# New ranks, longer charges for some loads, and more zero matmuls in an attention and MoE kernel ordered by a planner

## The chip, the cores and the metric

The kernel runs on one core of one Trainium2 chip. The metric is the device time of one execution in microseconds (us). The kernel before takes 373.11 us, the median of seven runs that lie between 372.59 and 374.45 us.

## The reference

The input is `q`, `k` and `v` of 8 batches x 8 heads x 576 positions x 64, a feature matrix `w_phi` (64 x 128), and the two weights of an MLP (512 x 2048 and 2048 x 512). All are float32, and so is the output.

```python
def phi(x):
    proj = np.einsum('bhsd,df->bhsf', x, w_phi)
    proj = proj - np.max(np.abs(proj), axis=-1, keepdims=True)
    return np.concatenate([np.exp(proj), np.exp(-proj)], axis=-1)
q_p, k_p = (phi(q), phi(k))
kv = np.einsum('bhsf,bhsd->bhfd', k_p, v)
z = np.sum(k_p, axis=2)
num = np.einsum('bhsf,bhfd->bhsd', q_p, kv)
den = np.einsum('bhsf,bhf->bhs', q_p, z)[..., None] + 1e-06
attn = num / den
...
x = attn.transpose(0, 2, 1, 3).reshape(B * S, H * D)   # 4608 x 512
h = x @ w_in
g = np.where(h > 0.0, h, np.exp(np.minimum(h, 0.0)) - 1.0)
return g @ w_out
```

It is linear attention with an exponential feature map, and behind it a two-layer MLP with ELU on every token.

## The kernel before

**Work and tiles.** Attention is cut into 16 quads of four heads: quads 2b and 2b+1 hold batch b. The MLP is cut into nine chunks of 512 tokens: chunk b takes the first 512 positions of batch b, and chunk 8 takes the last 64 positions of all batches (the "tails"). A chunk can start when both quads of its batch have delivered their part of `x`.

**One quad.** TensorE (PE) transposes k and q (L537, tails L541), multiplies them with `w_phi` (L565, L583 for the maxima, L714 and L726 for the transposed q features). VectorE (DVE) reduces the maxima `m_k`, `m_q` (L592). ScalarE (ACT) makes the exponentials `EK`, `EKt`, `Eq`, `Eqt` (L629, L765). From `m_k` ACT makes the scales `em` (L661), and GpSimd (POOL) multiplies `v` with them into `vs` (L684). PE then makes `kv` (L797), an engine copies it (L816), PE makes the outputs `pn` and `pnt` (L850, L865), DVE weighs and adds them into `tot` (L885, L891), divides (L923, L924) and multiplies `tot` with the reciprocal into `x` (L928; on DVE for quads 0 and 1, on POOL for the others). `x` is transposed into `xT` (L980 and L988 for batches 0 and 1, by DMA for later ones).

**One chunk.** For each of 16 column tiles: four matmuls into `ph` (mm1, L1031), `exp` on ACT (L1043), minus one on POOL (`u_sb`, L1047), the ELU on DVE (`gT`, L1054). Then 16 groups of matmuls into `po` (mm2, L1097), a copy (L1120) and a store.

**Loads.** k, q and the weights are read as float32, cast to bfloat16 on the way, and issued from POOL's own instruction stream (L385, L391, L412, L422). For batches 0 and 1 v is issued there too; for later batches it goes through SP. Batch 0 comes in halves of four heads plus tails (`load_first`, L1174); batch 1 comes whole plus tails (`load_kq`, L1192, with n = 0, 1, 2 for k, q, v).

**What sets the order.** All instructions are put in order when the kernel is built, by the class `Planner` (L125). Every piece of work is an `Op` with a charged duration for each engine that may run it, the ops that it waits for, and the PSUM banks that it takes. `run` (L169) is a list scheduler: it steps through a time of its own, and whenever an engine is free it takes, among the ops that are ready by the charges, the one with the lowest rank. Each engine later runs its list strictly in that order, waiting on semaphores for real. The charges therefore set the order only, never the time. The ranks are a table of 2091 numbers, `RANKS`: op n has the two digits 2n and 2n+1 in base 64.

A load is charged by its size; it is taken to have landed at

```python
took = o.load / self.MB_PER_US
o.seen = max(o.end + o.alone, dma + took + self.LANDING)
dma = max(dma, o.end) + took
```

with 0.37 MB per us, so that loads queue behind each other. At most eight loads of POOL are on their way at once (`AHEAD`, L140; `wait`, L207).

**Zeros in the gaps.** When PE starts an op after having stood idle in the planner's time, and that time is below 60 us, the planner first puts in matmuls of zeros into an otherwise free PSUM bank (`fill`, L1244 and L1247; the count is set at L264). One is taken as 0.056 us (`FILL`), and they are given half of the gap. They cost nothing in the planner's time. Ahead of everything else, 30 are put in at L1252.

Of the kernel before, what the change touches and what calls it, by code (L numbers as in the profile page):

```python
# [31 lines left out]

DIGITS = "0123456789ABCDEFGHIJKLMNOPQRSTUVWXYZabcdefghijklmnopqrstuvwxyz+-"
RANKS = (
    "0S0Y0b0a0n0X0c0v0o0w0-0z382k1x1t3H3B3y1v3o1n3J3Y3h3-784G4c080Q1i1b0B6v3K1Y7t1k0T"
    "2Q0P7a7h0s150t7c1o851w197T7g1+2c1l0G0A2t1z2A5w3PA81u060h0O0g3L0N2z096r0p033p9T0D"
    "2v211K4q39516z165V4L32233f2w0F302m4r3q6s704J8YA62C4N2g5D1D120K0e1N3v2r5q3N1U9u7M"
    "298I86272EBY8N7z839i0+AZAB7q8S375e2M8G898R6a5+6u3M049G130502013QBmPUTNBz7QVz758n"
    "8B601I2s6A0u0f3r0y0k280j1H1O0R0d2F1d0Z2+1f0q1RIC5T0U3k1A5k3n1L1P492H182o5848340i"
    "4t365p2L4n1y3F114Y461cAy4x4U4Q26509a3W5G5d3t5m5KDo633D5nBH3I9-3m5H424j8W5C3u1a3C"  # L40
    "F+2n1M2X524F1m1EAl6D1Z53656KDwE27I4H4i9EI+6F7G3e4h9X5lAE7UCT4W9O9SG+5XCeAC7E3X0l"
    "17003i3sAU3O547K0M774wCu9h7OAF1p9b4v7W7oCp7u7jA4Ah901-AgAj828c0r933R2b8z0HKH2-1C"
    "3T9y5a61DnA-Ao3a3l5M249D2S3Z0m5i4E2y764g2p3w4k1Q144I5o1T4o2e0V4K312i4l2x3zDe7H6o"
    "3b5W6y1F3E7J3S7P7b0C2U0J0I7m8r8k8p2I0E2K7s877x9n9r5u4e8dFv5y8m5PCJD63U7wA22a5R8b"
    "5Q3V7X7+5s5t6E6m6LCL8F0L6C6H416B2u4m1gFa4z0xEE6-CjAv95109f4s1B6l6i2P3344405I4a6M"
    "Ab3G5A9J3jBF725B5U926b6k2Z254XA33d2dBT9V5fCVAq6G3c984ZChGr7ZEF4PAe5S5Z6hEZBXBuCo"
    "CZ994B3+Bs8w4p9mBg8OAmCiCfBVHdB4IxBbGDFcBp7NG3CnB0ALBvDWBCAfI2GcF-ETFKEP5vDGAkH0"
    "BDHDDxD-EaAQDc7L7D3x8Q2V9s1J1e2W202J4T5b7n2O1j9vAD7i9l8C5NBnBJBSCm8Z7VDCCFAA7k7e"
    "CG8i4CD98q9pFD668M2NNsEiE7As8a6d2RCaBoAN1q1s1X5YC6CK4D4b436O0W6Z5F1V5h4d9R5j7r2f"
    "Gg6g9gCs2j1hAYEBAX35FfAJ4A2h4S6Q6P4OCvC3DO7p6q6jD8CXC98hC06w6n8T6tD1739B8xBiIR7A"  # L50
    "Cy7Y8X2D6S741r5x079A8+6URA9K9Z9k9U7B5c2G795L71CQ6p6+8LBA9MH98j1WHJ629xC284BUFr47"
    "2qGiF55-6fARI4DMMKAnGyDPJX7FCHEUCb594VDN5gAHLzDKJ-BGFBB9JY5EHn9CCYAxDj9NCc5JJj9c"
    "Hp2YG1DRHo2lMJArCx55RZ9+JNBMJnDSD4BWHfDDCw4-LeASJb8uLdB8Hl8yQZF7FoGUFEBP819FJGFl"
    "FdD0B5ApGICkC-DU8HI0KjFLH+KXFp4y4+4f7f64It4RCMCD6I6RCgCzCWC8888PC4B+8K9w8fCrAV9t"
    "809qKqOpE-AGA5AO2BDiDtB6B76WCSCA6e8DEKIK6TBtBZ1G5zB1DvDY9o6NDIELCEAK8U5rC+227CAM"
    "CRH4ClM+9WAT9P9L8g1S9dD594A7FzGG458A4M8e6VEYJHRCEvPDOoKrGCJz7lRBMyRNKxKtLLL3JL8J"
    "IP69EeB3ERByAIEN6XQ-KN9j6xF8GE6YK+PRBx6cB2CdFeRG97Fu7yDaFyC78tEVEHHCA+DV96ErFTK1"
    "9QIU9eEIDmFUC1KOD7FIHaBBBl2TOmE6J27vTkF6HkBfGqElJ7BqLiDEJZBRMtFJGpBcTFFCI83AHYFw"
    "A056SlFiHmB-G-F2Jl57UUFgJh8sUgFXI9BEOfG8K4BrQ1HZJi4uQFIcGlBKHIHAJ6BeD+GjPYIYNoEq"
    "CtFnMoGRLwIODqOQJ5E+KlCPE5JcLvJwGeHeG6E4CNEs7-DkE8BID3A1CCFNFHNCPLQI9zPKEgR7MuCU"  # L60
    "PqDgOTCO5ODACBRuKzL1ESAuNIL0MiKuKWFRQPJRCqIk8EDpFSC5QKNLInIjI6FFA9IaDFG5GHDXFq7R"
    "G7EC8vHEEDEzGBH-H3G9FZAdHtDdH1F9DLITLPFb679YE1CIFPF19IP4PAE3LFPJUNFkTOE0N+SFNWP3"
    "DhKCBkP2GOGLKcDfEoEtS7SUFOL6QbSSEpEG8VFQDZL48-KoHyTlGfOUFVEmLYIgAWGo9HHbFAH5LaK3"
    "HBF3FYAiGnDQHhL9JqGxGuOcFtGbMNLtJaBjMEIHM0GdMHJ0MjGMQ0I-IwAtQCLRIsAPQDIVHrBwQ9Nc"
    "JTNfSfKwJmFxPBK2Hz91QzIGIFBNGzJJO8GYUSLOIEBOT+LINyBQMQJQJ4AaQ3L-K5FhHcIvRtGNMGJO"
    "OWNDO6JMIZLhKFMgRFINJAQUN1LHMeSvHFOMMAKvO3KPP58oBdF0EyPvNFGwJ1EMI1HNAwOnIqMrKZOs"
    "KyKgP0N4N8K-N7EfKKEQO5EbKGIJGPSLOxFMFsS6EAHQQxN2DBIX6JPfHOPFUCEjDuIDS4HjEkDHHuH6"
    "LXAcIoGQHKBaHGJSGZOVJBDbH7IpLTGvI3DJGmT6IMSCEOGKHgJ8AzIrHPEuOYEJKEJrJkKLJxKSR0RE"
    "L7MzJoJ9PXQvKIRYSRKRNjP6TnPzRjRiHRDsJuR3NmJKKbHSIfJfQwSnOZS9JFJpIiRoLlI77dOOSyGs"
    "DlM6HHVuODGtDTKkIuGSOAKJD2OzGTIWIAFmP-NKT4MfQ2MlSzBhQYLyQOLqLpOdSbVqSdNVJWFjMSMp"  # L70
    "QsG4QyNQUOMYU4MFUiGaNvMqQfW4TzO2NRVrN0LQT1GVLfPlScO9QGMCUvW9SjN9U2NMQ5NUN-GWRvMO"
    "JULgUBLkRnPPMULmQkMmQoLbNHSmIzQeLMRJUIOwTuQnMsSgSGI5R57SEdEhFGReR9KhIyH8JEHVLUEW"
    "OSRxRaQqE9JsT5RzGAKTN6Q+NqSETET3JtRrFWSpRkRsP+IbJvHXL5T8JIILL8PcKAKsJCKdRqKeTQLo"
    "KpLWVmMXMILsMBO4MkHqVGK9HxUwLxHsVOJVHvVeLuDrOkMvRwPwGhRUHMMLG0KQHUF4KaJyPnRXKfPj"
    "ROV6VkRTQrTxNSDyNbLCNZNdPTQhUmNeIIEwIQL2HWRbRcOtNkKnNgKBPOOr8lSIPmMPNwPNTMKYOuLr"
    "QVM9OPMhToVWO7UVVaP1VTSaNhUXKiHLTmVVMnKmRyPSTaK7UZBLM5PWTLGkUkONUdMaOgOvO0OyUHNt"
    "J3U-QANPQiVLNpOXUbGJPrNEV3MDMwLDK6V2UENaJ+VIO+OROKSWMRPZMZV-L+O-URW1M4LZUjVRSeRH"
    "K0RdU9NzTYQ8ShRfPpRIWgNlUqRVSTSJWcQtUzPIW0UPSYSAU+UpOlUDVAWGUtLBKDNOLNUlMVEXPuH2"
    "M3OFKUUTTSTKR-RRTBUKRgR+T9RWR6PHR1TvLVEcIhDzGXLJLSIeIlQES2OIRDPxTTSiSOSHOHU3LKEn"
# [45 lines left out]
class Planner:  # L125
# [43 lines left out]
    def run(self):  # L169
        free = dict.fromkeys(self.LAG, 0.0)  # L170
# [11 lines left out]
        now = 0.0  # L182
# [53 lines left out]
        while todo:  # L236
            started = False
            for e in ready:
# [22 lines left out]
                for x in o.cost:  # L261
                    ready[x] = [y for y in ready[x] if y[1] is not o]
                if e == "PE" and 0.0 < free[e] and now < self.FILL_UNTIL and banks:
                    n = int(0.5 * (now - free[e]) / self.FILL)  # L264
                    if n:
                        if filled not in banks:
                            filled = min(banks, key=banks.get)
                        self.fill(filled, n)
# [50 lines left out]
def kernel(  # L319
# [10 lines left out]
    nc = tc.nc  # L330
# [140 lines left out]
    def plan_quad(i):  # L471
# [454 lines left out]
        def x_head(e, c):  # L926
# [8 lines left out]
        div = add({"DVE": 0.37}, divide, tots, key=-9.0)  # L935
        ops["x"] = [
            add(
                {"POOL": 1.11} if i > 1 else {"DVE": 0.68},
                lambda e, c=c: x_head(e, c),
                [div, *old("x_out")],  # L940
                key=-9.0,
# [232 lines left out]
    def load_first(n, part):  # L1174
        if part == 1:
            load((0, n, 1), 0.13, 1.26, lambda e: load_tails(nc.gpsimd, n, 0))
            return
        h = 2 * part

        def load_half(e):  # L1180
            load_main(nc.gpsimd, n, 0, h, h + 4)
            if not n and not part:
                make_identity(nc, ident)

        load((0, n, part), 0.52, 0.8 if n or part else 1.19, load_half)

    for n, part in (
        (0, 0), (0, 1), (0, 2), (1, 0), (1, 1), (2, 0), (2, 1), (1, 2), (2, 2)
# [1 line left out]
        load_first(n, part)  # L1190

    def load_kq(n):  # L1192
        load((1, n, 0), 1.05, 0.9, lambda e: load_main(nc.gpsimd, n, 1, 0, 8))
        load((1, n, 1), 0.13, 1.26, lambda e: load_tails(nc.gpsimd, n, 1))
        landed[1, n, 2] = landed[1, n, 0]

# [87 lines left out]
```

## Time and profile before

| | before |
|---|---|
| median of seven runs | 373.11 us |
| the profiled execution's own time | 372.99 us |
| its span, first to last instruction | 371.2 us |
| busy: PE / ACT / DVE / POOL | 352.2 / 271.9 / 266.8 / 248.5 us |
| PE busy with zeros (L1247), 212 matmuls | 20.6 us |
| first matmul of mm1 (L1031) starts | 51.1 us |
| mean DMA rate in the first 60 us | 202 GB/s |

Times in the profile run from the start of the span. Outside the span lie 372.99 - 371.2 = 1.8 us. In the tables by stretch of time, each engine has its busy time and, in brackets, the number of its instructions; "PEclk" is the share of full clock that TensorE was granted. In a chain of waits, each row has its start, its duration and what the end was waiting for at that moment. Matmuls are pipelined: the duration of one includes its way through the array.

### The profile page before, as it was taken

To read this page: it belongs to the slowest core of one execution; us is meant where nothing else is said; L and a number is where in the kernel's file an instruction comes from. 1 tells how busy PE (TensorE), PEld (TensorE's weight loads), DVE (VectorE), ACT (ScalarE), POOL (GpSimd) and SP (SyncE) were. 2 spreads that over 40 slices of the span, in tenths; PEclk is the share of its full clock that TensorE was granted. 3 is DMA by queue.
4 is the path that set the end of the run, shared out by engine and by line. 5 is a ranking of instruction groups with operands and counts; after the bars stand their busy time and mean duration, and the time that the engine had idled before them with its cause. 6 is when DMAs were issued, how large, how long until landed. Compare 5 with 4: busy or idle time off the path is not lost.

```text
span 371.2 us, 8974 instructions
## 1 busy us (share of the span) xinstructions
PE 352.2 (95%) x3380; PEld 197.0 (53%) x3426; DVE 266.8 (72%) x562; ACT 271.9 (73%) x601; POOL 248.5 (67%) x359
## 2 busy tenths in 40 slices
PE   7787989999998999999999999999999999999995
PEld 6566855555545454444554555464544554444444
DVE  4789789998879867868885889798858851777000
ACT  2998897988899945899678979996699733665111
POOL 8899989877967877689357794928485624675000
PEclk9999899999999999999999999999999999999999
DMA  8999999599794998757579353583120034000213
GB/s 130 212 193 238 210 201 213 35 130 177 100 169 69 179 224 127 135 117 143 119 92 186 91 143 83 135 175 63 34 60 2 34 86 118 1 0 2 86 57 87
DMA packets 85788, 43.20 MB, mean 116 GB/s; under 512 B 54704, under 2 KB 79664, under 8 KB 85744
## 3 DMA queue, kind: packets, MB, share of 16 engines
q1 hardware_dynamic: 56016, 26.10, 33.0%
q0 software_dynamic: 29328, 16.00, 31.6%
q8 instruction: 27, 0.44, 0.5%
q10 hardware_dynamic: 400, 0.52, 0.4%
q14 instruction: 17, 0.14, 0.1%
HBM read 36.77 MB, written 9.44 MB: 124 GB/s over the span
## 4 chain that ended last, share of the span: by engine, by line
PE 79%; POOL 8%; DMA 5%; issue 3%; ACT 3%; DVE 2%; POOLq 0%; ACTq 0%
PE po L1097 33%; PE ph L1031 29%; PE pkv L797 5%; PE pk L583 4%; PE pn L850 4%; DMA q_b<-in_q_dram 3%; POOL vs L684 3%; POOL u_sb L1047 2%; DMA k_b<-in_k_dram 2%; PE pq L714 1%; DVE gT L1054 1%; POOL w_in_sb L385 1%; PE pnt L865 1%; ACT EK L629 1%; POOL k_b L422 1%
## 5 line engine op out<-in xcount | busy, mean ns | idle before, releaser
L1097 PE MATMUL po<-w_out_sb,gT 128*128 128x512 bf16 (+1 forms) x567 | 130.8, 373 | 1.6 <-issue 0.6
L1047 POOL TENSOR_SCALAR u_sb<-e_sb 128x512 bf16<-128x512 f32 x144 | 87.9, 618 | 48.3 <-ACT e_sb L1043 45.1
L1031 PE MATMUL ph<-xT,w_in_sb 128*128 128x512 bf16 x491 | 118.3, 379 | 1.7 <-DVE gT L1054 0.5
L1054 DVE SCALAR_TENSOR_TENSOR gT<-u_sb,ph 128x512 bf16<-128x512 bf16 x144 | 96.2, 682 | 32.7 <-POOL u_sb L1047 32.4
L1043 ACT ACTIVATE e_sb<-ph 128x512 f32<-128x512 f32 x144 | 87.2, 618 | 31.0 <-PE ph L1031 27.1
L1031 PEld LDWEIGHTS <-w_in_sb 128*128 128x128 bf16 x576 | 53.7, 98 | 62.0 <-issue 4.2
L1097 PEld LDWEIGHTS <-gT 128*128 128x128 bf16 x592 | 54.0, 98 | 56.9 <-issue 2.9
L684 POOL TENSOR_TENSOR vs<-v_b,em 128x512 bf16<-128x512 f32 (+1 forms) x96 | 78.7, 844 | 1.6 <-DMA v_b<-in_v_dram 1.4
L629 ACT ACTIVATE EK<-pk 128x512 bf16<-128x512 f32 x128 | 68.8, 631 | 11.9 <-PE pk L583 11.5
L765 ACT ACTIVATE Eq<-pq 128x512 bf16<-128x512 f32 x128 | 70.2, 628 | 3.1 <-PE pq L714 3.0
L592 DVE TENSOR_REDUCE m_q<-pk 128x4 f32<-128x512 f32 (+1 forms) x80 | 48.4, 628 | 14.0 <-PE pk L583 10.9
L592 DVE TENSOR_REDUCE m_k<-pk 128x4 f32<-128x512 f32 (+1 forms) x80 | 47.6, 627 | 5.6 <-PE pk L583 4.6
L928 POOL TENSOR_TENSOR x<-tot,rec 128x576 bf16<-128x576 f32 x28 | 31.8, 1151 | 25.3 <-DVE rec L924 21.2
L1120 ACT COPY o_sb<-po 128x512 f32<-128x512 f32 (+1 forms) x28 | 16.1, 575 | 36.9 <-PE po L1097 34.7
L885 DVE TENSOR_TENSOR tot<-pn,w 128x260 f32<-128x260 f32 x64 | 26.1, 422 | 9.8 <-PE pn L850 7.4
L850 PEld LDWEIGHTS <-Eq 128*128 128x128 bf16 x512 | 22.2, 98 | 8.9 <-issue 1.2
L891 DVE TENSOR_TENSOR tot<-tot,pn 128x260 f32<-128x260 f32 x64 | 25.6, 418 | 0.4
L850 PE MATMUL pn<-kv,Eq 128*128 128x65 bf16 x512 | 25.3, 195 | 0.5 <-DVE gT L1054 0.4
L629 ACT ACTIVATE EKt<-pk 64x256 bf16<-64x256 f32 x64 | 22.9, 378 | 2.3 <-PE pk L565 1.2
L797 PEld LDWEIGHTS <-EK 128*128 128x128 bf16 x512 | 22.2, 98 | 3.5 <-issue 0.3
L797 PE MATMUL pkv<-vs,EK 128*128 128x65 bf16 x512 | 23.7, 195 | 0.2 <-POOL vs L684 0.2
L1247 PE MATMUL fill<-zeros 128*128 128x128 bf16 x212 | 20.6, 245 | 3.0 <-DVE zeros L1163 1.0
(75 smaller groups left out, 305.4 us busy)
## 6 DMA issues: line engine op xcount, KB each, us to landing
out_dram<-o_sb SPq DMA_DIRECT2D x32, 256.0 KB, 2.7
v_b<-in_v_dram SPq DMA_DIRECT2D x6, 1024.0 KB, 7.3
k_b<-in_k_dram POOLq DMA_DIRECT2D x7, 512.0 KB, 7.4
q_b<-in_q_dram POOLq DMA_DIRECT2D x7, 512.0 KB, 9.5
w_in_sb<-in_moe_w_in_dram POOLq DMA_DIRECT2D x8, 256.0 KB, 8.6
w_out_sb<-in_moe_w_out_dram POOLq DMA_DIRECT2D x4, 512.0 KB, 11.8
v_b<-in_v_dram POOLq DMA_DIRECT2D x2, 512.0 KB, 6.1
v_b<-in_v_dram POOLq DMA_DIRECT2D x1, 1024.0 KB, 11.6
```

The source lines that it names most:

```text
L592: nc.vector.tensor_reduce(largest(n)[:, cols], bank.tile[:, 0:len(range(2 * NS)[cols]), :], axis=AX.X, op=ALU.max, apply_absolute_value=True,)
L629: nc.scalar.activation(EK()[:, 2 * c + par, sg, :] if c < 2 else EKt[r, s, sg, :], bank.tile[r, 0:n, :].rearrange("p a b -> p (a b)"), ACT ...
L684: nc.gpsimd.tensor_tensor(st["vs"][:, sg, r, 0:D], kqv[b, 2][:, o:o + n * D].rearrange("p (n d) -> p n d", d=D), st["em"][:, sg, r, None]. ...
L765: nc.scalar.activation(dst, src, ACT.Exp, scale=1.0 - 2.0 * sg)
L797: nc.tensor.matmul(pkv[:, c, sg, :], st["EK"][:, 2 * c + t % 2, sg, (2 * s + t // 2) * F:(2 * s + t // 2 + 1) * F,] if t < NT else EKt[:, ...
L850: nc.tensor.matmul(pt[:, t, :], st["Eq"][:, par, c, sg, o:o + P], st["kv"][:, s, c, sg, :], start=True, stop=True,)
L928: (nc.vector if e == "DVE" else nc.gpsimd).tensor_tensor(tile("x", work, [P, NS, 2, D], BF16)[:, :, c, :], tot[:, r, 0:D], st["rec"][:, r, ...
L1031: nc.tensor.matmul(ph, w_in_sb[:, ct, jt * P:(jt + 1) * P], xTs[ch][:, ct, :] if ch < B else xT_tail[:, ct // 2, :, ct % 2, :], start=(ct ...
L1043: nc.scalar.activation(t["e"], bank.tile, ACT.Exp)
L1047: nc.gpsimd.tensor_scalar(t["u"], t["e"], -1.0, 1.0, op0=ALU.add, op1=ALU.mult)
L1054: nc.vector.scalar_tensor_tensor(gTs[ch][:, jt, :], t["u"], 0.0, bank.tile, op0=ALU.min, op1=ALU.max)
L1097: nc.tensor.matmul(bank.tile, gTs[ch][:, jt, tt * P:(tt + 1) * P], w_out_sb[:, jt, o0:o1], start=(jt == 0), stop=(jt == N_JT - 1),)
```

## The change

Four kinds of edits are made.

- The size charged for loads rises: k and q halves of batch 0 from 0.52 to 0.55, v halves of batch 0 from 0.52 to 0.62, v of batch 1 from 1.05 to 1.35. The bytes that are moved stay the same.
- `x` on DVE (quads 0 and 1, two ops each) is charged 1.05 us in place of 0.68.
- Zeros take 0.65 of a planned gap in place of 0.5.
- All of `RANKS` is replaced. It has the same 2091 entries, again each number from 0 to 2090 once.

No op is added or removed apart from the zero matmuls.

```diff
 RANKS = (
-    "0S0Y0b0a0n0X0c0v0o0w0-0z382k1x1t3H3B3y1v3o1n3J3Y3h3-784G4c080Q1i1b0B6v3K1Y7t1k0T"
...
+    "1B1g0S0V1V0-2c1-2b2j2x3K32312I303P3R4Z334A393S3g343h5Q1K1Z123i2F2-0w4S0X0D0M01A1"
...
                 if e == "PE" and 0.0 < free[e] and now < self.FILL_UNTIL and banks:
-                    n = int(0.5 * (now - free[e]) / self.FILL)
+                    n = int(0.65 * (now - free[e]) / self.FILL)
                     if n:
...
             add(
-                {"POOL": 1.11} if i > 1 else {"DVE": 0.68},
+                {"POOL": 1.11} if i > 1 else {"DVE": 1.05},
                 lambda e, c=c: x_head(e, c),
...
-        load((0, n, part), 0.52, 0.8 if n or part else 1.19, load_half)
+        load((0, n, part), 0.62 if n == 2 else 0.55, 0.8 if n or part else 1.19, load_half)
...
-        load((1, n, 0), 1.05, 0.9, lambda e: load_main(nc.gpsimd, n, 1, 0, 8))
+        load((1, n, 0), 1.35 if n == 2 else 1.05, 0.9, lambda e: load_main(nc.gpsimd, n, 1, 0, 8))
         load((1, n, 1), 0.13, 1.26, lambda e: load_tails(nc.gpsimd, n, 1))
```

## The prediction

> **What bounds the kernel now.** I read the table by stretch of time first: start, length, then busy time of PE, PEld, DVE, ACT and POOL, then granted clock, DMA share and GB/s.
>
> ```profile
> 0.00:10.00 10.00, 7.75 (x77) 7.02 (x77) 5.32 (x14) 2.92 (x5) 8.86 (x18) 1.00 0.86 133
> 10.00:20.00 10.00, 7.27 (x107) 5.48 (x106) 7.98 (x16) 9.61 (x23) 8.27 (x13) 1.00 1.34 211
> 20.00:30.00 10.00, 8.81 (x165) 6.91 (x164) 8.21 (x17) 9.93 (x27) 9.22 (x15) 1.00 1.18 202
> 30.00:40.00 10.00, 7.28 (x134) 6.03 (x131) 8.18 (x20) 7.40 (x20) 9.20 (x13) 0.87 1.22 230
> 40.00:50.00 10.00, 8.56 (x144) 7.22 (x142) 9.42 (x23) 9.43 (x23) 9.97 (x13) 0.96 1.37 207
> 50.00:100.00 50.00, 49.41 (x529) 27.44 (x534) 44.55 (x98) 43.09 (x98) 42.15 (x61) 1.00 1.02 138
> 100.00:120.00 20.00, 18.75 (x216) 10.67 (x218) 15.45 (x34) 18.46 (x45) 15.15 (x23) 1.00 0.80 122
> 120.00:340.00 220.00, 217.32 (x1893) 112.51 (x1924) 165.65 (x343) 165.41 (x358) 144.37 (x207) 1.00 0.50 99
> 340.00:371.20 31.20, 27.06 (x139) 13.68 (x140) 2.06 (x3) 5.69 (x11) 1.31 (x3) 1.00 0.22 68
> ```
>
> From 50 us on PE is full: it misses 0.59 + 1.25 + 2.68 = 4.5 us of 290, and 4.1 us at the end. Before 50 us it is busy 39.67 us, but about half of that is zeros:
>
> ```profile
> L1247 PE MATMUL fill<-zeros 128*128 128x128 bf16 x212 | 20.6, 245 | 3.0 <-DVE zeros L1163 1.0
> ```
>
> All but some 0.5 us of these lie before 50 us, so the first 50 us hold about 19.6 us of needed PE work and lose 30.4. The span is then 331.6 needed (352.2 - 20.6) + 30.4 + 0.5 + 4.5 + 4.1 = 371.1 of 371.2. What a new order can win is in the ramp, and there it is set by the start of mm1, at 51.1 us. Next, the chain of waits ahead of it (start, duration, what):
>
> ```profile
> 25.05 10.46 DMA q_b<-in_q_dram
> ...
> 35.56 0.24 PE trt L541
> ...
> 36.14 0.49 PE fill L1247 x6
> 36.63 1.54 PE pkv L797 x40
> ...
> 40.14 0.90 PE fill L1247 x9
> ```
>
> PE stands on the tails of q of batch 1, then on zeros, and only then makes kv of quad 1. Why that kv was not possible sooner is in POOL's timeline:
>
> ```profile
> 29.61 0.81 POOL L391 DMA_DIRECT2D w_out_sb<-in_moe_w_out_dram  x1
> 30.42 0.61 POOL L385 DMA_DIRECT2D w_in_sb<-in_moe_w_in_dram  x1
> 31.04 1.42 POOL L684 TENSOR_TENSOR vs<-v_b,em 128x128 bf16<-128x128 f32 x2
> 32.39 0.95 POOL L412 DMA_DIRECT2D q_b<-in_q_dram  x1
> 33.36 2.05 POOL L684 TENSOR_TENSOR vs<-v_b,em 128x512 bf16<-128x512 f32 x2
> ```
>
> vs of quad 1 ends at 35.41 us because POOL issues loads in between; its EK and Eq were finished by 30.3 us.
>
> **What the Trainium skill says.** "TensorE: Matmul & The Clock Gate", Part 1: after an idle window of about 3.4 us TensorE runs at half clock until it has been busy that long again. The trace agrees: 30 zeros take 3.38 us at the start (0.113 each), 24 take 1.50 us when warm (0.056 each plus 0.16 of way through the array), and the clock falls to 0.87 just after the stand at 33.9 to 35.6 us. Same page, "Step-by-step: what each phase is for": matmuls stay in program order and only weight loads are pulled ahead. The trace agrees: L541 idles PE for 1.48 us on a landing. "DMA: Bandwidth & Descriptors", "Queues, rings and completion order": a ring's descriptors are consumed in order. Here the q tails, 128 KB of input, need 10.46 us because v of batch 1 was issued before them (23.52, landing 11.6 us later). "SBUF — State Buffer", "SBUF: two separate sides": a DVE operation with two SBUF inputs and a GpSimd operation that reads SBUF exclude each other. `x` on DVE is such an operation (0.744 to 0.885 us, median 0.754).
>
> **The change, part by part.**
>
> *Charges.* At 0.37 MB per us, the new sizes put what lands after v of batch 1 later by 4 x 0.03/0.37 + 2 x 0.10/0.37 + 0.30/0.37 = 0.32 + 0.54 + 0.81 = 1.7 us in the planner's time. The landings say that this is the right direction: v of batch 1 landed 3.9 us after the load before it (31.17 to 35.08), q of batch 1, with as many elements, 2.6 us after the one before it; the charge goes from 2.84 to 3.65. So the planner no longer believes that the q tails come before kv of quad 1, and the 1.48 us stand has no reason to be planned. Behind it stood six zeros that waited 0.30 us for a bank (ACT reading `qT`) and took 0.49. But kv could not start before vs, at 35.41; it started at 36.42. Worth 1.0 us.
>
> *Clock.* From 36.6 to 41.7 us needed work ran cold: 40 of pkv 1.54 against 1.26 us later, 8 of pk 0.61 against 0.40, 2 of pq 0.64 against 0.38, 16 of pn about 0.2 over: 0.95 us. Without the stand, and with more zeros, I take half: 0.5.
>
> *Zeros.* The 182 in gaps stand for at least 182 x 0.056/0.5 = 20.4 us of planned gap. At 0.65 they become about 240: 58 x 0.056 = 3.2 us more of PE time warm, 58 x 0.113 = 6.5 cold. It costs nothing where PE waits anyway (1.09 us after the group at 15.76, 0.77 at 11.65, 1.48 at 33.86) and everything where real work is ready. Two groups stand on the chain; at 1.3 times they add 2 x 0.056 + 3 x 0.12 = 0.5 us. Bounds: -1.4 us (the whole cold stretch saved: 0.95 and 0.4 of its zeros) to +3.2 (all on the path). Value taken: +0.4.
>
> *Ranks.* Decoded, the vs of quad 1 had 382 to 539 against loads at 226 (w_out), 235, 242 (w_in) and 251 (q of batch 2); now it has 36 to 222 against 234, 196, 266 and 304. Its scales (L675) go from 150 to 233, so some loads still pass. `x` of quad 1 goes from 349 and 1164 to 245 and 163, against maxima of quad 3 that were at 19, 146, 485 and 502 and are now at 285, 526, 12 and 495. The eight large EK of quad 2 go from 22 to 824 to between 27 and 1300, six of them above 600. Batch 0 is thus preferred to batch 1. How far can that pull mm1? POOL gave 0.65 + 0.64 + 0.93 + 1.25 + 0.59 + 0.81 + 0.81 + 0.61 + 0.95 = 7.2 us to loads between the scales and the last vs of quad 1, so vs could end at 28 us; ACT caps it at 30.3. Then DVE caps it: quad 0's `x` is done at 37.8, quad 1 needs 10 operations of about 0.4, a divide of 0.5 and 1.5 for `x`, then 0.6 of transposes and 1.0 of copy: 45.4, or 5.7 us sooner. A third of this, since ACT and DVE carry the work of batch 1 in the same time: -1.9. The loads delayed for it are covered by up to eight on their way; if that cover fails, w_in or w_out hold mm1 or mm2 by up to the 0.9 us of an issue each.
> The first loads turn to k of heads 4 to 7 (28), q (31), v (63), k of heads 0 to 3 (75). The identity for the transposes is issued with the last of these; three loads earlier than it cost about 0.8 us each, so it is there at about 5.2 us, ahead of the first landing at 5.58. Nothing. q of batch 0 lands some 3 us sooner and k tails some 3 us later; ACT is full either way. Nothing.
> `x` at 1.05 only moves what is planned after it: nothing.
> The rest of the order is new too. In the full stretch POOL waits once for v (1.44 us ahead of 108.73), and PE loses 1.25 us between 100 and 120. v of later batches keeps its charge, so this can come or go: taken at +1.0, between -1.2 and +3.
>
> Sum: -1.0 - 0.5 + 0.4 - 1.9 + 1.0 = -2.0. Span 369.2, with the 1.8 around it 371.0; the profiled execution (372.99) stands 0.12 below the median of 373.11. **Predicted: 371.0 us.**
>
> **The rivals.**
> - *Only exchanged waits, 372.9.* ACT is busy 9.6, 9.9, 9.4 of 10 us in three of the ramp's stretches, POOL above 9, DMA full. If ACT's and DVE's sum rather than the order of batch 0 sets when PE fills, mm1 starts sooner but with less of batch 1 done, and only about 0.2 is left. Against it: ACT idles 2.6 us from 30 to 40.
> - *Slower, 375.0: POOL stands at a vs whose v has not landed.* POOL is in order; minus one of the MLP is queued behind, then the ELU, then the bank, then PE. One such stand costs 1.25 us here. With vs ranked ahead, more can come. The rest of the sum is -3.0, so it decides from the third stand on (3.75); four cost 5.0 and leave +2.0. For it speaks that v of later batches keeps its charge; against it that the trace has only one such wait.
> - *Large gain, 367.5.* The full 5.7 us of the pull: -1.0 - 0.5 + 0.4 - 5.7 + 1.0 = -5.8. Against it: DVE is at 9.4 of 10 from 40 us.
> - *The change does nothing* is excluded: the order of the first loads alone differs.
>
> **How the numbers follow.** Chances: forecast 0.60 (own range 369.4 to 372.3), exchanged waits 0.15, slower 0.19, large gain 0.06. The range of 368.8 to 374.2 leaves out most of the large gain and half of the slower case, and takes in the bounds of zeros and of the steady stretch around the forecast. What a measurement can tell from no change is 0.2%, 0.75 us: faster is below 372.4, slower above 373.9. Faster: 0.58 + 0.06 + 0.03 = 0.67; same: 0.02 + 0.10 + 0.02 = 0.14; slower: 0.02 + 0.17 = 0.19.
>
> **What would show it.** Right: mm1 (L1031) starts before 50 us; vs of quad 1 ends before 33; no wait near 1.5 us of L541 on q; clock above 0.9 from 30 to 40; about 270 zeros. Wrong: PE losing over 6 us from 100 to 340, POOL's waits for v above 3 us, or zeros above 3 us in the chain before mm1.

## The result

The kernel after takes 373.88 us (median of 27 runs, 373.22 to 375.92). The kernel before, run beside it, takes 373.85 us (64 runs, 371.49 to 376.26). The ratio is 1.0012, with a 95% interval of 0.9998 to 1.0026: no change that can be told. The forecast of 371.0 us was wrong.

Executions of one kernel differ by more than 1%, and a profile is one of them: its span can lie a microsecond or two from the median. So ratios and their intervals decide on times, and profiles only on where the time is. Medians here are of all executions of a kernel, while ratios leave out those that lie more than 1.5% above its fastest one.

| | before | after |
|---|---|---|
| the profiled execution: time / span | 372.99 / 371.2 us | 373.33 / 371.5 us |
| busy with zeros | 20.6 us, 212 | 23.5 us, 280 |
| last two q tails of batch 1 landed | 35.51 us | 34.40 us |
| last `vs` of quad 1 ends | 35.41 us | 35.41 us |
| last `x` of quad 1 ends | 49.05 us | 45.55 us |
| first matmul of mm1 starts | 51.13 us | 50.48 us |
| MLP matmuls by 60 us, counted by their weight loads | 32 | 28 |
| the same by 120 us | 217 | 221 |

The table by stretch of time of the kernel after, in the columns of the one before (start, length, busy time of PE, PEld, DVE, ACT, POOL, granted clock, DMA share, GB/s):

```profile
20.00:30.00 10.00, 8.98 (x175) 7.47 (x173) 8.24 (x16) 9.83 (x25) 9.98 (x16) 1.00 1.01 159
30.00:40.00 10.00, 8.36 (x166) 7.00 (x163) 9.19 (x25) 9.36 (x26) 9.94 (x15) 1.00 1.17 247
40.00:50.00 10.00, 7.23 (x122) 5.92 (x122) 6.73 (x17) 6.24 (x14) 9.35 (x14) 1.00 1.30 210
50.00:100.00 50.00, 49.05 (x521) 27.65 (x530) 45.15 (x98) 42.86 (x101) 40.95 (x60) 1.00 0.99 158
100.00:120.00 20.00, 19.66 (x228) 11.54 (x230) 16.35 (x38) 14.67 (x36) 15.51 (x24) 1.00 0.64 87
120.00:340.00 220.00, 217.67 (x1897) 112.66 (x1929) 166.54 (x345) 164.40 (x357) 143.78 (x206) 1.00 0.53 98
```

The clock no longer falls between 30 and 50 us, but now PE, DVE and ACT are all less busy from 40 to 50 us. The zeros, in the groups of the page:

```profile
L1247 PE MATMUL fill<-zeros 128*128 128x128 bf16 x280 | 23.5, 234 | 5.0 <-ACT Eq L765 1.7
```

PE is busy 40.46 us before 50 us (39.67 before), 23.1 of them zeros, so 17.4 us are needed work (19.6 before, 0.95 of which were the cold stretch's surcharge). So mm1 starts 0.65 us sooner, but by 50 us PE has done 1.2 us less of the work that it has to do. The span adds up as the forecast's did: 330.8 needed (354.3 - 23.5), 32.6 lost in the ramp (30.4), 0.4 of later zeros, 3.6 lost from 50 to 340 us (4.5) and 4.1 at the end: 371.5. The ramp loses 2.2 us more; against that stand 0.95 of needed work that is no longer cold and 0.9 in the steady stretch.

One part of these losses isn't real. The traces of both kernels lack records of the MLP's matmuls: they hold 1056 (after) and 1058 (before) of 1104, and a missing record reads as idle time. The trace of `after_act_less`, a later experiment in the order of the kernel after, has all 1104 and loses 1.0 us from 60 to 340 us, against 3.5 in the kernel after. So PE is even fuller from mm1 on than the 3.6 and 4.5 us say.

The chain of waits ahead of mm1, again start, duration, what:

```profile
27.58 6.82 DMA q_b<-in_q_dram
...
34.44 0.23 PE trt L541
...
43.21 0.77 PE fill L1247 x11
43.98 0.33 PE pk L583 x8
...
44.60 1.58 ACT Eq L765 x3
46.18 0.04 issue
46.22 1.33 PE fill L1247 x21
47.56 0.34 PE pk L583 x7
...
49.26 0.56 PE fill L1247 x7
...
50.48 0.38 PE ph L1031
```

It still runs through the q tails at L541. In the kernel before the same line was:

```profile
35.56 0.29 PE L541 MATMUL trt<-ident,q_b 128*128 128x128 bf16 x2 [1.48 <-DMA q_b<-in_q_dram]
```

The stand has gone from 1.48 to 0.09 us: PE comes to the tails 0.3 us later, and they have landed 1.1 us sooner. mm1 starts 0.65 us sooner. From the landing to mm1 the chain takes another 16 us. Twelve groups of zeros take 5.0 us of it; 21 of these zeros wait 1.69 us until ACT's `Eq` are done, and quad 3's keys (L583, at 47.56) stand behind them. `x` of quad 1 is ready at 45.55 us (the last of the four `x` on DVE starts at 44.8 and takes 0.75), but its transposes stand behind those keys and start at 48.50. First the four `x` (durations in ns, first and last start), then PE:

```profile
L928 DVE TENSOR_TENSOR x<-tot,rec x4: 741/746/751, 36.7 to 44.8; 128x576 bf16<-128x576 f32 x4
46.22 1.33 PE L1247 MATMUL fill<-zeros 128*128 128x128 bf16 x21 [1.69 <-ACT Eq L765]
...
48.50 0.61 PE L980 MATMUL tr<-ident,x 128*128 128x128 bf16 x8
```

POOL's timeline shows why `vs` of quad 1 is no sooner:

```profile
19.39 0.34 POOL L675 CAST vs<-em 128x36 bf16<-128x36 f32 x1 [1.77 <-ACT em L661]
19.57 3.40 POOL L684 TENSOR_TENSOR vs<-v_b,em 128x512 bf16<-128x512 f32 x4
22.93 0.64 POOL L385 DMA_DIRECT2D w_in_sb<-in_moe_w_in_dram  x1
...
30.63 4.78 POOL L684 TENSOR_TENSOR vs<-v_b,em 128x512 bf16<-128x512 f32 x6
```

The loads no longer cut quad 1's products apart, but they stand ahead of them. Quad 0's scales also come later: POOL waits 1.77 us for them and makes them at 19.39 in place of 14.75 us. This is in line with k of heads 0 to 3 being loaded fourth, so that it lands at 10.91 in place of 5.58 us; that it is the cause was not tested.

### The profile page after: what moved, and what is told of

Same layout as the page of the kernel before. It is cut to its first block, busy times and chain, and to the rows that moved or that the text cites. A ratio compares the mean times of both kernels' runs of the same rounds, so it can differ in the third digit from the quotient of the medians.

```text
span 371.5 us, 9103 instructions
## 1 busy us (share of the span) xinstructions
PE 354.3 (95%) x3446; PEld 200.0 (54%) x3494; DVE 269.3 (72%) x570; ACT 267.0 (72%) x593; POOL 247.0 (66%) x359
## 3 DMA queue, kind: packets, MB, share of 16 engines
q1 hardware_dynamic: 56016, 26.10, 32.6%
## 4 chain that ended last, share of the span: by engine, by line
PE 79%; ACT 6%; POOL 6%; DMA 3%; issue 3%; DVE 3%; POOLq 0%; ACTq 0%
PE po L1097 33%; PE ph L1031 27%; PE pk L583 4%; PE pkv L797 4%; PE pn L850 3%; POOL vs L684 2%; ACT Eq L765 2%; POOL u_sb L1047 2%; DMA q_b<-in_q_dram 2%; PE fill L1247 2%; ACT EK L629 2%; PE pq L714 2%; DVE gT L1054 1%; DMA k_b<-in_k_dram 1%; ACT e_sb L1043 1%
## 5 line engine op out<-in xcount | busy, mean ns | idle before, releaser
L1097 PE MATMUL po<-w_out_sb,gT 128*128 128x512 bf16 (+1 forms) x568 | 132.4, 373 | 1.4 <-issue 0.2
L1043 ACT ACTIVATE e_sb<-ph 128x512 f32<-128x512 f32 x144 | 86.3, 610 | 34.2 <-PE ph L1031 32.1
L684 POOL TENSOR_TENSOR vs<-v_b,em 128x512 bf16<-128x512 f32 (+1 forms) x96 | 77.1, 832 | 0.1
L765 ACT ACTIVATE Eq<-pq 128x512 bf16<-128x512 f32 x128 | 69.2, 625 | 6.9 <-PE pq L714 6.8
L1120 ACT COPY o_sb<-po 128x512 f32<-128x512 f32 (+1 forms) x27 | 15.6, 576 | 40.2 <-PE po L1097 39.9
L1247 PE MATMUL fill<-zeros 128*128 128x128 bf16 x280 | 23.5, 234 | 5.0 <-ACT Eq L765 1.7
L1247 PEld LDWEIGHTS <-zeros 128*128 128x128 bf16 x280 | 19.0, 105 | 8.2 <-issue 6.4
```

The lines of the kernel that those rows point to most:

```text
L684: nc.gpsimd.tensor_tensor(st["vs"][:, sg, r, 0:D], kqv[b, 2][:, o:o + n * D].rearrange("p (n d) -> p n d", d=D), st["em"][:, sg, r, None]. ...
L765: nc.scalar.activation(dst, src, ACT.Exp, scale=1.0 - 2.0 * sg)
L1043: nc.scalar.activation(t["e"], bank.tile, ACT.Exp)
L1097: nc.tensor.matmul(bank.tile, gTs[ch][:, jt, tt * P:(tt + 1) * P], w_out_sb[:, jt, o0:o1], start=(jt == 0), stop=(jt == N_JT - 1),)
L1247: nc.tensor.matmul(t[:, 0:P], zeros, zeros, start=True, stop=True)
```

## The experiments

Ranks and charges were not tried apart: the ranks fit one set of charges, and with the other set the planner finds no order. Where an experiment moves or doubles single ops, everything else keeps its place in the order. Each ratio is to the kernel before, run on the same chip at the same time, with its 95% interval. The kernel after was not run beside them; it stands at 1.0012 from runs of its own, so a comparison with it carries both intervals.

### The zeros

The count of zeros in gaps is changed and nothing else; the 30 at the start stay. `after_zeros_0`, `after_zeros_050`, `before_zeros_0` and `before_zeros_065` use f = 0, 0.5, 0, 0.65:

```diff
-                        self.fill(filled, n)
+                        n = int(f * (now - free[e]) / self.FILL)
+                        if n:
+                            self.fill(filled, n)
```

> The new kernel without the zero matmuls in gaps (the 30 at the start stay; same order, same banks). Theory Z, zeros stand on the way to mm1: about 3 us of them lie in the chain from 42 to 50.5 us, so mm1 starts near 48 and the time falls by 1.5 to 3 us against the new kernel. Theory C, zeros are needed for the clock: the granted clock falls below 0.9 in the stretches from 10 to 40 us, the ramp's needed matmuls take up to twice as long, and the time rises by 1 us or more. Theory O, the order exchanged waits for waits and zeros are hidden: within 0.5 us.

> The new kernel with zeros for half of a planned gap, as before (185 in gaps in place of 250), same order and banks. Z: a quarter of the 3 us goes, -0.7 us. C: the clock stays full as in the kernel before or dips to 0.87 in one stretch, 0 to +1 us. O: no change, within 0.3 us.

> The kernel before with zeros for 0.65 of a planned gap alone (234 in gaps in place of 182). Z: +0.4 to +0.8 us, since two groups on its chain grow by 2 and 3. C: the dip of the clock to 0.87 between 30 and 40 us goes away, -0.5 to -1 us. O: no change, within 0.3 us.

> The kernel before without zeros in gaps (the 30 at the start stay). Z: the 1.4 us of zeros in its chain go, -1 us. C: clock near 0.5 to 0.7 from 10 to 45 us and +1.5 us or more. O: within 0.5 us.

`after_zeros_until_40`:

```diff
-                        self.fill(filled, n)
+                        if now < 40.0:
+                            self.fill(filled, n)
```

> The new kernel, same order and banks, zeros only in gaps before 40 us of the planner's time (about 42.5 us real): the 11, 21, 4, 7 and 6 zeros in front of mm1 go, 2.7 us with the way through the array. Theory Z with C, zeros in front of mm1 cost and those before it keep the clock: mm1 starts at 48.4 to 49 us with a clock above 0.95, and the time falls by 1.5 to 2 us against the new kernel. Theory O, the order sets it whatever the zeros do: within 0.5 us.

| | median us | ratio | mm1 starts | MLP matmuls by 60 us |
|---|---|---|---|---|
| after_zeros_0 | 373.72 | 1.0003 (0.9987 to 1.0019) | 48.40 | 28 |
| after_zeros_050 | 373.23 | 0.9993 (0.9971 to 1.0016) | 49.87 | 28 |
| after_zeros_until_40 | 373.22 | 0.9981 (0.9960 to 1.0002) | 47.80 | 28 |
| before_zeros_065 | 373.78 | 1.0009 (0.9987 to 1.0031) | 49.69 | 38 |
| before_zeros_0 | 373.89 | 1.0007 (0.9990 to 1.0025) | 53.33 | 24 |

Taking all zeros out of the gaps, or changing their share, moves the time by no amount that can be told. In the new order zeros delay mm1 by up to 2.7 us, and in the profiled executions without them the cold clock takes that back. The one that may gain is `after_zeros_until_40`: it stands 0.31% below the kernel after, some 1.2 us, and with both intervals that is 0.2 to 2.1 us. It is the largest of several differences, so it isn't sure. The timeline of PE in `after_zeros_until_40` (start, duration, instruction, and in brackets the idle time before it):

```profile
47.80 0.58 PE L1032 MATMUL ph<-xT,w_in_sb 128*128 128x512 bf16 x1 [0.30 <-DVE xT L989]
48.61 2.77 PE L1032 MATMUL ph<-xT,w_in_sb 128*128 128x512 bf16 x6 [0.22 <-issue]
...
52.28 1.04 PE L538 MATMUL tr<-ident,q_b 128*128 128x128 bf16 x8
```

The same in the kernel after:

```profile
50.48 1.89 PE L1031 MATMUL ph<-xT,w_in_sb 128*128 128x512 bf16 x7
...
52.84 0.61 PE L537 MATMUL tr<-ident,q_b 128*128 128x128 bf16 x8
```

Seven matmuls of mm1 take 1.89 us warm; here the same seven spread over 3.58 us. Of 2.68 us of lead 0.56 are left at the next transposes, 2.4 us of warm matmuls later, and by 60 us both kernels have begun 28 matmuls of the MLP. This execution had a mean clock of 0.990. Eight of the 22 had about 0.995 and took 372.0 us in the mean, against 373.9 of the thirteen near 0.990: the clock does not always take the lead back.

### Single waits in PE's order

`before_kv_first`: in the kernel before, the transposes of the two q tails and the six zeros behind them go behind kv of quad 1, so that PE can't stand on the landing ahead of kv.

```diff
+        n = pe.index(op[363])      # q tails, L541
+        x = pe[n:n + 3]
+        del pe[n:n + 3]
+        n = pe.index(op[163]) + 1  # kv of quad 1
+        pe[n:n] = x
```

> The kernel before, but the two transposes of the q tails of batch 1 and the six zeros behind them stand behind kv of quad 1, so that the 1.48 us stand is no longer ahead of it. The prediction's step (kv at 35.4 in place of 36.4 us): -1.0 us. Theory O, other waits take its place: within 0.3 us; kv starts at 35.5 us in both cases.

`after_x_first`: in the kernel after, the main transposes of `x` of quad 1 and their copy go ahead of quad 3's keys (two banks change places for it, and the four zeros ahead of the transposes fall away).

```diff
...
+        n = pe.index(op[185])                        # x transposes of quad 1
...
+        del pe[n - 1:n + 1]
+        pe.insert(pe.index(op[320]) + 1, op[185])
+        dve.remove(op[187])                          # their copy
+        dve.insert(dve.index(op[368]), op[187])
```

> The new kernel, but the transposes of x of quad 1 and their copy stand ahead of the keys of quad 3 (four zeros between them go, and two PSUM banks change places from there on). They can start when x is there, 45.6 in place of 48.5 us. Theory Q, PE's order in front of mm1 gave the gain back: mm1 starts at 48.5 to 49.5 in place of 50.5 us, and the time falls by 1 us or more. Theory O: within 0.5 us, since the keys of quad 3 come as much later.

`before_72_more`, and later `after_72_more`: 72 more zeros right ahead of the first matmul of mm1.

```diff
+        n = pe.index(op[189]) - 1
+        pe[n][1] += 72
```

> The kernel before with 72 more zero matmuls just ahead of the first matmul of mm1, nothing else moved: 72 x 0.0556 = 4.0 us of PE time. Theory P, PE is full from mm1 on and its start sets the end (the premise of the prediction): +3.5 to +4 us. Theory S, something else sets the pace of the ramp (loads, or the sums of ACT and DVE), and PE catches up behind mm1: less than +2 us.

> The changed kernel with 72 more zeros right ahead of the first matmul of mm1: 72 x 0.056 = 4.0 us more for PE at about 50 us. In the kernel before the same zeros cost about 2.7 us. If PE has the same slack behind mm1's start in the changed kernel, 2.7 us again, 376.6. If mm1's start sets the end, as the forecast had it, all 4.0: 377.9. If in the changed kernel mm1 starts early but then waits for other work, as the 28 matmuls of the MLP by 60 us in all its variants hint, less than 2: below 375.9.

| | median us | ratio | mm1 starts |
|---|---|---|---|
| before_kv_first | 374.84 (374.72 for 21 of 22) | 1.0022 (0.9998 to 1.0045) | 49.43 (51.13 before) |
| after_x_first | 374.23 | 1.0015 (1.0000 to 1.0030) | 49.96 (50.48 after) |
| before_72_more | 378.03 (376.62 for the nine of eleven that the ratio counts) | 1.0073 (1.0037 to 1.0109) | 54.00 |
| after_72_more | 378.26 | 1.0134 (1.0095 to 1.0173) | 54.98 |

`before_kv_first` is the forecast's first step made alone, and it works as far as mm1: no stand at L541, kv starts at 34.90 in place of 36.47 us, mm1 1.70 us sooner. Not all of the 1.70 us is the stand's. This execution was granted full clock from 30 to 50 us, and the profiled one of the kernel before was not. `before_72_more` (below) had full clock there too, and the stand; its mm1 starts at 54.00 us behind 4.0 us of added zeros, so at about 50.0 without them. By this estimate the clock accounts for 1.1 us and the edit for 0.6. The time is not better. The chain of `before_kv_first` a little later:

```profile
48.61 14.72 DMA k_b<-in_k_dram
63.33 0.05 issue
63.38 0.23 PE trt L608
```

and its timeline of PE (L608 is L541 of the kernel before):

```profile
60.47 0.61 PE L604 MATMUL tr<-ident,k_b 128*128 128x128 bf16 x8
63.38 0.23 PE L608 MATMUL trt<-ident,k_b 128*128 128x128 bf16 x1 [2.30 <-DMA k_b<-in_k_dram]
```

PE stands 2.30 us for the k tails of batch 2. In the kernel before it comes to the same place at 62.61 us, and the last of those tails has landed at 62.44, 0.17 us earlier:

```profile
62.61 0.22 PE L541 MATMUL trt<-ident,k_b 128*128 128x128 bf16 x1
```

The 1.70 us are given back there in full; some of the 2.30 us is due to the tails themselves, which landed at 63.33 us in this execution. `before_zeros_065`, also at full clock, shows the same: mm1 1.44 us sooner, then 1.11 us of waiting on the k tails at 62.43. What stands behind mm1's start in the kernel before is a landing.

`after_x_first` took little: PE then waits 1.07 us for `x`, the tail transposes and thirteen zeros still come after the keys, and mm1 starts 0.5 us sooner. Even these 0.5 us don't come from the edit: the second of the q tails' transposes (L541) is 0.5 us sooner in this execution too (34.33 in place of 34.84 us), and from it to mm1 it is 15.63 us, as in the kernel after (15.64).

The two runs with 72 zeros show that a later mm1 is paid for. 72 zeros are 4.0 us of PE time; in the profiled executions mm1 starts 2.9 us later in the kernel before and 4.5 us later in the new order. The time rises by 2.7 us (1.4 to 4.1) and by 4.6 us (3.1 to 6.0, taking 1.0012 as exact). So later costs most or all of it, while sooner brought nothing sure.

### More work for one engine in the ramp

Single ops of the kernel after are done twice, writing the same numbers again.

```diff
+        for x in [x for x in seq["ACT"] if x.cost == {"ACT": 0.48} and 16.0 < x.end < 32.0][::4]:
+            def twice(e, f=x.fn):
+                f(e)
+                f(e)
+            x.fn = twice
```

DVE has `{"DVE": 0.6}`, 16 to 32, `[::2]`; POOL has `{"POOL": 1.0}`, 16 to 33.5, `[::3]`.

> The changed kernel with six exponentials of ACT (four EK and two Eq, planned between 16 and 32 us) done twice, the second time writing the same numbers: 6 x 0.49 = 2.9 us more for ACT in the ramp, all else in its order. If the ramp is limited by the amount of work of ACT, which is busy 9.8 of 10 us from 10 to 30 us (the rival of exchanged waits), the whole 2.9 us come through: 376.2 to 376.9. If single waits in PE's order up to mm1 set the end (the premise of the forecast), the part of them that stands before mm1 comes through, less than 1.5 us: 374 to 375.3.

> The changed kernel with five reductions of the maxima on DVE (planned between 16 and 32 us) done twice: 5 x 0.60 = 3.0 us more for DVE in the ramp. DVE is busy 8.2 to 9.2 of 10 us from 10 to 40 us, so some 3 us of it are idle: if the amount of work limits the ramp, DVE is the second after ACT, and 1 to 2 us come through, 374.8 to 376. If single waits set the end, less than 1.5 us.

> The changed kernel with three of the products vs on POOL (planned between 16 and 33.5 us) done twice: 3 x 1.06 = 3.2 us more for POOL, and all loads behind them are issued that much later. POOL is busy 9.9 of 10 us from 20 to 40 us, and the chain of waits ahead of mm1 runs through POOL to the issue of the q tails. If POOL's row of vs and loads limits the ramp, 3 us come through: 376.5 to 377. If ACT does, POOL's delay is hidden to more than half, below 1.5 us: 374 to 375.3.

| | work added | median us | ratio |
|---|---|---|---|
| after_act_3_more | 2.9 us | 377.11 | 1.0103 (1.0075 to 1.0131) |
| after_dve_3_more | 3.0 us | 375.38 | 1.0063 (1.0042 to 1.0085) |
| after_pool_3_more | 3.2 us | 377.05 | 1.0108 (1.0077 to 1.0139) |

Less 1.0012, that is 3.4, 1.9 and 3.6 us: within the intervals, work on ACT or POOL comes through whole, and work on DVE to about two thirds. Taken alone this looks like an ACT-bound or POOL-bound ramp, the form that the rival of exchanged waits gave it. But all three additions act at the same place. In `after_act_3_more` (L608 stands for L541) the tails have landed at 35.35 us, and PE comes to them late:

```profile
37.60 0.22 PE L608 MATMUL trt<-ident,q_b 128*128 128x128 bf16 x1
```

In the two others PE comes to them late as well, at 36.57 (DVE) and 37.99 us (POOL), with the landings at 35.38 and 36.04. In the kernel after PE came to the tails only 0.09 us before it could go on, so any work put in ahead of them makes it late. Whether an engine is the limit is told by taking work away.

### Less work for one engine in the ramp

The order stays that of the kernel after; only quads 0 and 1 do less. The lines that set the missing parts to zero are left out here.

```diff
 # after_dve_less: maxima over half of the features
-                bank.tile[:, 0:len(range(2 * NS)[cols]), :],
+                bank.tile[:, 0:len(range(2 * NS)[cols]), 0:F // 2 if i < 2 else F],
...
 # after_act_less: EK over half of its columns
+                dst = EK()[:, 2 * c + par, sg, :] if c < 2 else EKt[r, s, sg, :]
+                if i < 2 and c < 2:
+                    n, dst = 2, dst[:, 0:2 * F]
...
 # after_pool_less: vs for half of the positions
+                if i < 2:
+                    r, n = slice(c * NS, c * NS + NT), NT
...
```

`after_all_less` has all three.

> The changed kernel in the same order, with the sixteen large EK exponentials of quads 0 and 1 made over half of their columns (the other half is set to zero by DVE at the start, while it waits for the first loads): ACT does about 16 x 0.2 = 3 us less in the ramp, and half of those features of the keys are left out. If ACT's amount of work alone limits the ramp, some 2.5 to 3 us are gained: 370.5 to 371.3. If ACT, DVE, POOL and the landings limit it together, less than 1 us: 372.8 to 373.8.

> The changed kernel with the maxima of quads 0 and 1 on DVE taken over half of the features (the other half is left out): 16 large reductions at about 0.35 in place of 0.60 us, 4 us less for DVE. If DVE alone limits the ramp, 3 us or more are gained, below 371. If the limits are shared, less than 1 us.

> The changed kernel with the eight large products vs of quads 0 and 1 made for half of the positions (the rest is set to zero at the start; half of those v is left out): 8 x 0.5 = 4 us less for POOL, and the loads behind them are issued that much sooner. If POOL's row of products and loads alone limits the ramp, 3 us or more are gained, below 371. If the limits are shared, less than 1 us.

> The three together: ACT 3, DVE 4 and POOL 4 us less in the ramp, leaving out what the three leave out. If these engines' rows limit the ramp, together or one of them, 2.5 to 4 us are gained: 369.8 to 371.3. If PE's order and the landings of the loads keep it where it is, less than 1.5 us: above 372.3.

Medians: 374.68, 1.0023 (1.0004 to 1.0042) for ACT; 374.23, 1.0021 (1.0000 to 1.0041) for DVE; 375.14, 1.0042 (1.0026 to 1.0057) for POOL; 375.11, 1.0047 (1.0028 to 1.0067) for all. Only the one on DVE is clean. In the others DVE sets the missing parts to zero first, which takes longer than its idle time: its first copy of `kT` starts at 7.88, 7.89 and 10.04 us, against 6.85. So two were made again with ACT setting the zeros from 2.0 us on, where it has nothing to do until 8.56:

> The changed kernel with the eight large products vs of quads 0 and 1 made for half of the positions, 4 us less for POOL, and the missing part set to zero by ACT before its first exponential (four copies, 2 us, in an idle stretch of 6.5 us); half of those v is left out. If POOL's row of products and loads sets the ramp, as the ranks step of the forecast had it, mm1 starts 2 us sooner or more and 2 to 3 us are gained: 370.5 to 371.9. If not, less than 1 us: above 372.8.

> ACT 3, DVE 4 and POOL 4 us less in the ramp in the changed order, the missing parts set to zero by ACT in its idle stretch (eight copies, 5.8 us from 2.0 us on); it leaves out the same half of the keys' features, maxima and v of quads 0 and 1. If the three rows of work limit the ramp, 2.5 to 4 us are gained: 369.8 to 371.3. If PE's order with its zeros and banks and the landings of the loads hold it, less than 1.5 us: above 372.3.

`after_pool_less_2` takes 373.72 us, 1.0015 (0.9989 to 1.0042); `after_all_less_2` takes 373.97 us, 1.0011 (0.9990 to 1.0032). With 3, 4 and 4 us less on ACT, DVE and POOL the time is that of the kernel after. With both intervals, any of the clean three could hide a gain of about 1 us against the kernel after, and no more. At L541, PE's timeline now has waits. `after_dve_less`:

```profile
35.81 0.23 PE L541 MATMUL trt<-ident,q_b 128*128 128x128 bf16 x1 [1.04 <-DMA q_b<-in_q_dram]
36.21 0.22 PE L541 MATMUL trt<-ident,q_b 128*128 128x128 bf16 x1
```

`after_pool_less_2`:

```profile
35.10 0.23 PE L541 MATMUL trt<-ident,q_b 128*128 128x128 bf16 x1 [0.93 <-DMA q_b<-in_q_dram]
35.50 0.22 PE L541 MATMUL trt<-ident,q_b 128*128 128x128 bf16 x1
```

`after_all_less_2` (L543 stands for L541):

```profile
33.65 0.23 PE L543 MATMUL trt<-ident,q_b 128*128 128x128 bf16 x1 [0.68 <-DMA q_b<-in_q_dram]
34.05 0.22 PE L543 MATMUL trt<-ident,q_b 128*128 128x128 bf16 x1
```

and the kernel after, where there is no bracket, thus no wait of note:

```profile
34.44 0.23 PE L541 MATMUL trt<-ident,q_b 128*128 128x128 bf16 x1
34.84 0.22 PE L541 MATMUL trt<-ident,q_b 128*128 128x128 bf16 x1
```

The stand of the kernel before is back: what the engines save, PE waits for the tails. And from the second of these transposes to the first matmul of mm1 it is 15.64 us in the kernel after (34.84 to 50.48), 15.63 in `after_dve_less` (to 51.84), 15.63 in `after_pool_less_2` (to 51.13) and 15.62 in `after_act_less` (34.71 to 50.33): always the same, as long as the zeros are. With fewer zeros it is shorter, 14.71 us in `after_zeros_050` and 12.54 in `after_zeros_until_40`. In `after_all_less_2`, where the clock falls to 0.83 between 40 and 50 us, it is 17.1.

| | last q tail issued | landed | PE waits at L541 | mm1 starts |
|---|---|---|---|---|
| before | 25.05 | 35.51 | 1.48 | 51.13 |
| after | 27.58 | 34.40 | 0.09 | 50.48 |
| after_dve_less | 27.99 | 35.77 | 1.04 | 51.84 |
| after_pool_less_2 | 26.05 | 35.06 | 0.93 | 51.13 |
| after_all_less_2 | 25.16 | 33.60 | 0.68 | 51.16 |
| after_pool_3_more | 29.93 | 36.04 | 0.06 | 54.00 |

This is why mm1 starts where it does. Both orders have two such pieces ahead of it: the landing of batch 1's q tails at 33.6 to 36 us, which an issue 2.4 us sooner (25.16 against 27.58) moved by 0.8 us, and behind it some 16 us of PE's order with its zeros and its waits. The change brought the one 1.1 us forward and made the other 0.5 us longer. At an equal clock it is longer by more: the 15.6 us of the kernel before hold the cold stretch, and at full clock the same order takes 14.5 us (`before_zeros_065`, 35.15 to 49.69) or 14.7 (`before_72_more`, 35.30 to about 50.0), against 16.1 in the new order. By this estimate the 0.65 us by which mm1 starts sooner are owed to the clock of the profiled pair, and at an equal clock it would start some 0.5 us later. Work of quads 0 and 1 that is taken from an engine ends in front of the landing; work added to one reaches PE behind it and costs most or all of it.

These runs take work only from what is done ahead of the landing. From 34.8 to 50 us ACT is busy 10.70 of 15.2 us in `after_act_less` and 10.85 in the kernel after, since its work there belongs to batch 1. What less work of ACT and DVE behind the landing would bring wasn't tried, and no run brought the landing alone forward in the new order.

Also open is what the landing itself is limited by. In both kernels the DMA engines are named busy almost throughout, but in the new order the rate falls to 159 GB/s from 20 to 30 us (202 before), while POOL makes `vs` and issues no load between 17.6 and 22.9 us. No run moved fewer bytes or split the tails' queue, so neither bandwidth nor the place in the queue is shown to be the cause.

## Why the prediction was wrong

- **Charges, -1.0: this step failed.** The stand at L541 went as forecast, but the gain did not come with it. The step counted a stand as lost time because kv was queued behind it. In the kernel before, all that follows is again timed by a landing, the k tails of batch 2 at 62.44 us, with 0.17 us to spare: `before_kv_first` removed the stand alone; mm1 started 1.70 us sooner (about 0.6 of it from the edit, the rest from the clock), and PE lost 2.30 us at those tails. In the kernel after, q's tails still time a piece of PE's order that is longer than before (16.1 us from landing to mm1; 15.6 before, and some 14.6 at full clock). The rule that I gave in "what would show it" (no wait near 1.5 us of L541) was fulfilled, and proved nothing.
- **Ranks, -1.9: this step failed too.** `x` of quad 1 did come 3.5 us sooner. But mm1 came only 0.65 us sooner, and by the estimate above owes even this to the clock. PE's order sets quad 3's keys and 25 zeros ahead of the transposes; `after_x_first`, which moved the transposes alone, brought mm1 nothing, so the keys and zeros time it. The premise under it, that less in POOL's row of loads and `vs` starts mm1 sooner, was not borne out: `vs` of quad 1 still ended at 35.41 us (I had said before 33), and with 4 us less for POOL mm1 starts at 51.1 us.
- **The premise that the start of mm1 sets the end** holds in one direction. Later by 2.9 and 4.5 us cost 2.7 and 4.6 us. Sooner by 1.4 to 2.7 us in four other kernels gained nothing sure, at most some 1.2 us in `after_zeros_until_40`; in their traces the lead was spent on a cold clock (after_zeros_0, after_zeros_until_40) or at the next landing (before_kv_first, before_zeros_065). What the premise left out is how much of its needed work PE has done when mm1 starts: 1.2 us less by 50 us in the new order. `before_zeros_0` is an exception: its mm1 starts 2.2 us later, its ratio is only 0.07% above 1, at an interval of -0.10 to 0.25%.
- **Clock, -0.5, and zeros, +0.4.** In the profiled pair the clock rose from 0.87 to 1.00 from 30 to 40 us, and needed work is 0.95 us shorter; 280 zeros where I had said about 270. In part this is luck. I took the stand at L541 for the cause of the fall and for agreement with a window of about 3.4 us; it was 1.48 us long, and `before_72_more`, with the same order up to mm1 and a stand of 1.03 us there, was granted full clock from 30 to 50 us. Over all executions the direction holds: the mean clock is at least 0.997 in 11 of 28 of the kernel after and in 49 of 235 of the kernel before that ran beside the experiments. But these 11 take 373.55 us in the mean and those 49 take 372.78, so at an equal clock the new order looks slower; they come from several chips, and this wasn't tested by itself. For the zeros, 0.5 or 0.65 of a gap makes no difference that can be told in either order (before_zeros_065 at 1.0009; after_zeros_050 at 0.9993 against 1.0012).
- **Steady stretch, +1.0**: wrong in sign, within its bounds of -1.2 to +3. PE lost 0.9 us less there than before by the traces, nearly all of it between 100 and 120 us (1.25 against 0.34).
- **The sum.** Charges, ranks and zeros stood at -2.5 in the ramp; the ramp lost 2.2 us more instead. Less 0.95 (clock), 0.9 (steady stretch) and 0.1 (fewer zeros after 50 us) that makes +0.3 us, the rise of the span from 371.2 to 371.5.
- **The rivals.** "Only exchanged waits", 372.9 with a chance of 0.15, came nearest in time, and its picture fits: mm1 starts sooner, but with less done. Its reason, the amount of work of ACT and DVE, doesn't hold for quads 0 and 1 (`after_dve_less`, `after_all_less_2`); for the work of batch 1 behind the landing it is open. The slower rival (POOL at a `vs` without its v) did not happen: POOL waits for no v in the kernel after. The large gain's own sum, -5.8, gives 367.2 and not 367.5.
- **The signs.** Of the signs of being right, three came (no stand at L541, the clock, the zeros' number) and two did not (mm1 at 50.48 us, `vs` at 35.41). Of the signs of being wrong, one came: zeros take 5.0 us of the chain before mm1, where I had set 3.

## What to carry to other kernels

A stand on a landing is not lost time by itself: subtract it, then follow the engine to the next landing and see how much it has to spare there (here 0.17 us), since the gain is no larger than that unless this landing comes sooner too. Ask of each of two orders what single event times the work in question and how long the fixed piece behind it is; if both are the same, expect new ranks only to move the waits. Compare them at the same clock, and look at how much work is done when that event comes, not only at when it comes. Doubling work shows only that there is no slack to be late; whether an engine is the limit is told by taking work from it, and here, for the work ahead of the landing, that gave nothing on three engines at once.

## What the runs showed of the hardware

The clock fell without a long idle stretch, and came back late. In `after_zeros_0` PE's longest idle gaps between its first zeros and 20 us were 1.53, 0.79, 0.79 and, when it was long cold, 2.32 us. Its table by stretch of time:

```profile
5.00:8.00 3.00, 1.24 (x24) 0.90 (x24) 1.47 (x5) 0.25 (x1) 3.00 (x6) 1.00 1.22 246
8.00:10.00 2.00, 1.04 (x8) 0.77 (x8) 1.93 (x4) 2.00 (x5) 0.85 (x2) 0.57 1.56 199
10.00:13.00 3.00, 2.75 (x22) 1.57 (x22) 3.00 (x7) 3.00 (x7) 2.33 (x4) 0.50 1.50 208
13.00:16.00 3.00, 2.51 (x27) 1.75 (x26) 1.74 (x7) 1.86 (x5) 3.00 (x5) 0.50 1.10 232
16.00:21.00 5.00, 1.56 (x13) 0.90 (x10) 3.67 (x8) 4.78 (x16) 2.35 (x5) 0.50 1.50 207
21.00:25.00 4.00, 3.88 (x39) 2.91 (x38) 2.90 (x7) 3.61 (x10) 4.00 (x6) 0.50 0.90 150
25.00:28.00 3.00, 2.25 (x42) 1.77 (x42) 2.93 (x5) 3.00 (x7) 2.99 (x6) 0.94 0.90 119
```

It was granted half clock from about 8.3 us (0.57 in the mean from 8 to 10) to about 25 us, though PE was busy 5.26 of the 6 us from 10 to 16; it returned after 3.88 of 4 us. The Trainium skill, "TensorE: Matmul & The Clock Gate", Part 1, puts the fall after an idle window of about 3.4 us and the return after about as long of sustained work. The return agrees with that. The fall does not, if idle means one gap: here PE was busy 1.24 of 3 us ahead of it. Nor does the fall in the kernel before, with its stand of 1.48 us.

Loads issued by POOL landed in the order of their issue in both traces up to 50 us; in the kernel before v of batch 1 landed at 35.08 and the q tails behind it at 35.26 and 35.51 us. That fits the ring order by which the prediction explained the 10.46 us of the tails. The section that the prediction names for it says it of the queues of SP and ACT, while these loads are POOL's, and no run here took the tails out of their place.

The zeros that hold the clock cost about what they save, in both orders: with all of those in gaps and with none the ratios lie within 0.1% of each other (1.0003 against 1.0012; 1.0007 against 1, intervals as above).
